# Wider first loads, a later sink-score step and moved DMA transposes in a fused window-attention and SwiGLU kernel

## The chip, the cores and the metric

One core of a Trainium2 chip runs the kernel. The metric is the device time of one execution in microseconds (us); lower is better. Three runs of the kernel before gave 272.84, 273.07 and 273.93 us, the median is 273.07 us.

## What is computed

The reference, cut to what matters (B, H, S, D = 4, 8, 768, 64; 4 sink tokens, a window of 128; d_model 512, d_ff 1536; all f32):

```python
scores = (1.0 / np.sqrt(D)) * np.matmul(q, k.transpose(0, 1, 3, 2))
keep = (pos[None, :] < n_sink) | ((rel >= 0) & (rel < window))   # rel = query position - key position
a = softmax(np.where(keep, scores, -1e9))
attn = np.matmul(a, v)
x = attn.transpose(0, 2, 1, 3).reshape(B * S, H * D)
g = x @ w_gate
out = (g / (1.0 + np.exp(-g))) * (x @ w_val) @ w_out
```

Each query sees at most 128 keys of its window and the 4 first keys (the sinks) of its sequence.

## The kernel before

The 3072 tokens are 12 groups of 256 (three to each of the four sequences). The attention of a group g is a row of steps: `step_T` (L234) turns k and q to the layout [head dim, token] with TensorE transposes and evicts them into `kT`, `qT`; `step_S` (L275) makes the scores of the window, the exponentials on ScalarE (L297) and puts off a multiplication by the mask on VectorE (L302); `step_K` (L306) makes the scores of the sinks from `kss`, four keys per head that `step_ks` (L262) copied out of `kT`; `step_PV` (L318) multiplies by v and normalises into `xn`; `step_X` (L351) turns `xn` into `xT`, the input of the feed-forward part. From group 4 on, k, q and x are not turned on TensorE but by DMA transposes, all of them issued on SP's queue: `xbar(g)` (L253) issues four of them, from `nat` to `kT` and `qT`, and `step_X` one for each 128 tokens (L360).

The feed-forward part works on eight blocks of 256, 256, 256, 512, 512, 512, 512 and 256 tokens: `gate` (L373) for the two first products (`pg`, tanh in `th`, `pv`, then `u` and `ht` on VectorE), `down` (L406) for the last product, its eviction `ot` on ScalarE and the output's DMA on SP's queue (L424). Block 3 holds groups 3 and 4, block 5 groups 7 and 8.

The order of the work is written by hand. `weave(us, slots(...))` goes through a list of units (gates and downs) and calls the attention steps of a slot inside the unit with that number: in a gate between `pg` and `pv`, in a down between its matmuls. Each engine and each DMA queue works through its instructions in program order. Loads with a cast from f32 to bf16 are issued on POOL's queue in the order k and q of groups 0 and 1, v of group 0 (`va`), the first gate and value weights (`wg`, `wv`), and so on (L180 to L200). A DMA on POOL's queue takes one of eight semaphores in turn, and waits until the DMA that had it eight places earlier has landed; SP's and ACT's DMAs share eight others in the same way.

Group 0 is special. Its heads 0 to 3 (pairs 0 and 1 of two heads) are loaded as f32 by SP (k) and ACT (q), one DMA for each pair, and cast by VectorE (L517) and ScalarE (L518); pairs 2 and 3 are cast by four DMAs of POOL (`pair_by_cast`, L180). In all eight a partition holds four tokens of one head, the two heads of a pair stand in the two halves of the partitions, and the access pattern of the source has the two heads as its outermost dimension:

```python
return src[0, 2 * p:2 * p + 2, 0:256].rearrange("w (m r) d -> w m (r d)", r=4)
```

`pair_T` (L479) transposes a pair with sixteen 64x64 matmuls (L486). `fill` issues eight matmuls on zeros ahead of it.

Of the kernel before, what the change touches and what calls it, by code (L numbers as in the profile page):

```python
# [7 lines left out]
FP32 = mybir.dt.float32  # L8
BF16 = mybir.dt.bfloat16
# [5 lines left out]
def kernel(  # L15
# [12 lines left out]
    nc = tc.nc  # L28
    P = 128
    B, H, S, D = q.shape  # L30
# [22 lines left out]
    def pool(name, bufs, psum=False):  # L53
        if psum:
            return ctx.enter_context(
                tc.tile_pool(name=name, bufs=bufs, space=bass.MemoryType.PSUM))
        return ctx.enter_context(tc.tile_pool(name=name, bufs=bufs))

    const = pool("const", 1)
    wpool = pool("wpool", 1)  # L60
    rowp = pool("rowp", 3)
    natp = pool("natp", 3)
    stp = pool("stp", 4)
    vpool = pool("vpool", 1)
    kqtp = pool("kqtp", 2)
    epool = pool("epool", 2)
# [12 lines left out]
    def bank(shape, dtype, name):  # L79
        return psum.tile(shape, dtype, tag="b", name=name)  # L80


    rows, nats, vas = {}, {}, {}
# [8 lines left out]
    def new_rows(g):  # L92
        rows[g] = rowp.tile([P, 2, NP2, 4 * D], BF16, tag="rows", name="rows")
        return rows[g]

    def load_rows(g, pairs=ALL, tensors=(0, 1)):
        b, c = divmod(g, GC)
        x = rows[g] if g in rows else new_rows(g)
        for i in tensors:
            for w in range(2):  # L100
                nc.gpsimd.dma_start(
                    x[64 * w:64 * (w + 1), i, pairs],
                    by_rows((k, q)[i], b, w, pairs, c * 256))
# [39 lines left out]
    ident = const.tile([P, P], BF16)  # L143
# [20 lines left out]
    nc.vector.memset(kss, 0.0)  # L164


    def by_pair(src, p):
        return src[0, 2 * p:2 * p + 2, 0:256].rearrange("w (m r) d -> w m (r d)", r=4)

    new_rows(0)  # L170
    first = {}
    for p in range(2):
        for i, eng in ((0, nc.sync), (1, nc.scalar)):
            st = stp.tile([P, 4 * D], FP32, tag="st", name="st")
            eng.dma_start(st, by_pair((k, q)[i], p))
            first[p, i] = st
    nc.scalar.activation(warmed, one, AF.Exp)

    def pair_by_cast(p, i):
        nc.gpsimd.dma_start(rows[0][:, i, p], by_pair((k, q)[i], p))  # L180

    pair_by_cast(2, 0)
    nc.gpsimd.iota(tq, [[1, P]], base=0, channel_multiplier=0,
                   allow_small_or_imprecise_dtypes=True)
    nc.gpsimd.iota(tk, [[0, 1]], base=0, channel_multiplier=1,
                   allow_small_or_imprecise_dtypes=True)
    pair_by_cast(2, 1)
    pair_by_cast(3, 0)
    pair_by_cast(3, 1)
    load_rows(1)  # L190
    load_v(0)
    load_gate(0)
# [21 lines left out]
    for p in range(NP2):  # L214
        for w in range(2):
            h = 2 * p + w
# [12 lines left out]
    def new_T(b):  # L229
        if b not in kTs:  # L230
            kTs[b] = kqtp.tile([P, NP2, S], BF16, tag="kT", name="kT")
            qTs[b] = kqtp.tile([P, NP2, S], BF16, tag="qT", name="qT")
# [29 lines left out]
    def step_ks(b):  # L262
        for h in range(2):
            r = slice(h * D, (h + 1) * D)
            nc.vector.tensor_copy(
                out=kss[r, b, :, h * NS:(h + 1) * NS], in_=kTs[b][r, :, 0:NS])
        vsb = const.tile([P, H, D + 1], BF16, tag=f"vsb{b}", name="vsb")
        nc.vector.tensor_tensor(
            vsb,
            vcf[:, b:b + 1].broadcast_to([P, H, D + 1]),  # L270
            diag_h.rearrange("q (h o) -> q h o", o=1).broadcast_to([P, H, D + 1]),
            op=ALU.mult)
        vsbs.append(vsb)
# [32 lines left out]
    def step_K(g):  # L306
        b, c = divmod(g, GC)
        if c == 0:
            return
        ps = bank([P, 256], FP32, "pk")  # L310
        for p in range(NP2):
            nc.tensor.matmul(
                ps[32 * p:32 * p + KW], kss[:, b, p], qTs[b][:, p, c * 256:(c + 1) * 256],
                start=True, stop=True, skip_group_check=True)
        es_t[g] = espool.tile([P, 256], BF16, tag="es", name="es")
        nc.scalar.activation(es_t[g], ps, AF.Exp, scale=scale)
# [113 lines left out]
    def gates(tb):  # L430
        return [(gate, tb, f) for f in range(0, DFC, 512 // SIZES[tb])]

    def downs(tb):
        return [(down, tb, t) for t in range(SIZES[tb] // P)]

    def A(fn, *a):
        return lambda: fn(*a)

    def T(g):
        return [A(step_T, g, i, p2) for p2 in range(2) for i in range(2)]  # L440

    def Ss(g):
        return [A(step_S, g, p2) for p2 in range(2)]

    def PVs(g):
        return [A(step_PV, g, j, hh) for hh in range(2) for j in range(2)]

    def Xs(g):
        return [A(step_X, g, j) for j in range(2)]

    def K(g):
        return A(step_K, g)

    def weave(us, slots):
        assert all(i < len(us) for i in slots)
        for i, (fn, tb, x) in enumerate(us):
            fn(tb, x, slots.get(i, []))
# [7 lines left out]
    def slots(*pairs):  # L465
        sl = {}
        for at, steps in pairs:
            for i, step in zip(at if isinstance(at, tuple) else (at,) * len(steps),
                               steps):
                sl.setdefault(i, []).append(step)  # L470
        return sl
# [7 lines left out]
    def pair_T(p, key_eng):  # L479
        new_T(0)  # L480
        pt = bank([P, 2, 256], FP32, "pt")
        for i in range(2):
            for r in range(4):
                for w in range(2):
                    h = slice(64 * w, 64 * (w + 1))
                    nc.tensor.matmul(  # L486
                        pt[h, i, r:256:4], rows[0][h, i, p, r * D:(r + 1) * D],
                        ident[h, h], start=True, stop=True, skip_group_check=True)
        if key_eng == "a":
            nc.scalar.copy(out=kTs[0][:, p, 0:256], in_=pt[:, 0])  # L490
        else:
            nc.vector.tensor_copy(out=kTs[0][:, p, 0:256], in_=pt[:, 0])
        nc.vector.tensor_copy(out=qTs[0][:, p, 0:256], in_=pt[:, 1])
# [20 lines left out]

    fill(8, bank([P, 512], FP32, "w"))
    for p in range(2):
        nc.vector.tensor_copy(out=rows[0][:, 0, p], in_=first[p, 0])  # L517
        nc.scalar.copy(out=rows[0][:, 1, p], in_=first[p, 1])  # L518
        pair_T(p, "a")
    pair_S(0, 1)  # L520
    pair_T(2, "v")
    pair_S(1)
    pair_mask(0)
    pair_T(3, "v")
    pair_S(2, 1)
    pair_mask(1)
# [8 lines left out]
    masks1 = list(later)  # L535
# [13 lines left out]

    nc.vector.tensor_scalar(lt8, th8, float(NS), None, op0=ALU.is_lt)  # L550
    nc.vector.scalar_tensor_tensor(diag_h, th8, 0.0, lt8, op0=ALU.is_ge, op1=ALU.mult)
    for m in masks1[:2]:
        m()
    step_ks(0)
    for m in masks1[2:]:
        m()
    step_K(1)
    load_rows(3)
    load_v(3)

# [5 lines left out]
    def L(*fs):  # L566
        def f():
            for x in fs:
                x()
        return f  # L570

    weave(us, slots(
        (1, PVs(1) + Xs(1)),
        ((5, 5, 6, 6), T(2)), ((7, 8), Ss(2)), (8, [K(2)]),
        ((9, 9, 10, 10), PVs(2)), (11, Xs(2)),
        (12, [L(A(load_nat, 4), A(load_v, 4), A(load_nat, 5), A(load_v, 5),
                A(load_nat, 6), A(load_v, 6))]),
        ((13, 14, 15, 16), T(3)), ((17, 18), Ss(3)), (18, [A(step_ks, 1)]),
        (18, [A(xbar, 4)]),
        ((19, 19, 20, 20), PVs(3)), (21, Xs(3)),  # L580
        ((20, 21), Ss(4)), (21, [K(4)]), (22, [A(xbar, 5)]),
        ((22, 22, 23, 23), PVs(4)), (23, Xs(4))))

    def pair(ga, gb, sh=0):
        s = sh
        return [((s, s + 2), Ss(ga)), (s + 2, [K(ga)]),
                ((s + 4, s + 5, s + 6, s + 7), PVs(ga)),
                ((s + 6, s + 8), Ss(gb)), ((s + 8, s + 9), Xs(ga)), (s + 8, [K(gb)]),
                ((12, 12, 13, 13) if s else (10, 11, 12, 13), PVs(gb)),
                ((14, 14) if s else (13, 14), Xs(gb))]  # L590

    weave(gates(3) + downs(3), slots(
        (0, [L(A(load_nat, 7), A(load_v, 7))]), (2, [A(xbar, 6)]),
        (2, [L(A(load_nat, 8), A(load_v, 8))]), (5, [A(step_ks, 2)]), *pair(5, 6),
        (8, [A(xbar, 7)]), (9, [L(A(load_nat, 9), A(load_v, 9))]),
        (14, [A(xbar, 8)]), (14, [L(A(load_nat, 10), A(load_v, 10))])))
    weave(gates(4) + downs(4), slots(
        *pair(7, 8), (8, [A(xbar, 9)]), (9, [A(step_ks, 3)]),
        (9, [L(A(load_nat, 11), A(load_v, 11))]), (13, [A(xbar, 10)])))
    weave(gates(5) + downs(5), slots(*pair(9, 10), (6, [A(xbar, 11)])))  # L600
    us = gates(6) + gates(7) + downs(6) + downs(7)
    us[-1] = (lambda tb, t, a: down(tb, t, a, True), *us[-1][1:])
# [37 lines left out]
```

## Time and profile before

| | |
|---|---|
| median of three runs | 273.07 us |
| the profiled execution | 273.33 us |
| its span, first to last instruction | 271.5 us |
| PE busy | 240.5 us (89%) |
| VectorE busy | 165.6 us (61%) |
| ScalarE busy | 109.8 us (40%) |
| mean granted share of the TensorE clock | 0.987 |
| chain that ended last: PE, DVE, DMA, SP's queue | 74%, 9%, 9%, 3% |

The chain is followed back from the last instruction: at each step to what released it. A share of 74% for PE means that for 74% of the span the last thing to be waited for was a matmul; the rest is where another engine or a transfer was. A row of idle time names the engine that waited and what ended its wait.

### The profile page before, as it was taken

How to read it: one execution, taken by the hardware profiler on the slowest of the kernel's cores; microseconds unless marked ns; L12 is line 12 of the kernel's file. 1: busy time of each engine (PE TensorE's matmuls, PEld its weight loads, DVE VectorE, ACT ScalarE, POOL GpSimd, SP SyncE). 2: the span in 40 equal slices, each digit the busy share in tenths (PEclk: the TensorE clock that was granted, in tenths of full speed). 3: DMA queues.
4: the chain of work that ended last, by engine and by line, in shares of the span. 5: the costliest groups of instructions: out<-in, count | busy, mean ns of one | idle time of the engine just before them, and what ended most of it. 6: DMA issues, size and time to landing. Idle time of an engine off the chain costs nothing.

```text
span 271.5 us, 5112 instructions
## 1 busy us (share of the span) xinstructions
PE 240.5 (89%) x2016; PEld 138.4 (51%) x2039; DVE 165.6 (61%) x347; ACT 109.8 (40%) x213; POOL 71.1 (26%) x93
## 2 busy tenths in 40 slices
PE   5039679999999958999999999969999999999995
PEld 1026468877865523454444545424545445568543
DVE  4016977788686503899608899117898058977300
ACT  2016613733365414554138471235461265233122
POOL 8139665399450052491006100000000000000000
PEclk9999999999999997999999999988999999999999
DMA  3949999999995379999149910462010320000122
GB/s 35 127 50 145 190 187 206 203 161 150 128 156 70 114 133 197 151 145 115 58 116 163 130 39 4 108 186 57 0 39 2 116 77 2 19 22 0 39 91 105
DMA packets 102960, 27.38 MB, mean 101 GB/s; under 512 B 88985, under 2 KB 99993, under 8 KB 102937
## 3 DMA queue, kind: packets, MB, share of 16 engines
q0 software_dynamic: 72544, 13.91, 65.2%
q1 hardware_dynamic: 30132, 12.89, 20.3%
q8 instruction: 16, 0.26, 0.4%
q10 hardware_dynamic: 260, 0.26, 0.3%
q14 instruction: 8, 0.06, 0.1%
HBM read 28.34 MB, written 6.29 MB: 128 GB/s over the span
## 4 chain that ended last, share of the span: by engine, by line
PE 74%; DVE 9%; DMA 9%; SPq 3%; ACT 3%; issue 2%; DVEq 0%; ACTq 0%
PE pv L388 22%; PE pg L388 21%; PE pd L419 19%; DMA st<-in_k_dram 6%; PE o L336 4%; PE s L290 4%; DMA xT<-xn 2%; DVE ht L402 2%; DVE xn L342 2%; SPq L259 2%; PE pt L244 2%; ACT e L297 1%; DVE e L302 1%; DVE u L401 1%; PE pt L486 1%
## 5 line engine op out<-in xcount | busy, mean ns | idle before, releaser
L388 PE MATMUL pg<-xT,wg 128*128 128x256 bf16 (+1 forms) x380 | 75.3, 329 | 6.7 <-DMA xT<-xn 6.5
L395 ACT ACTIVATE th<-pg 128x512 f32<-128x512 f32 x72 | 43.4, 603 | 83.8 <-PE pg L388 83.3
L388 PE MATMUL pv<-xT,wv 128*128 128x256 bf16 (+1 forms) x374 | 74.9, 328 | 1.4 <-DVE ht L402 0.8
L401 DVE SCALAR_TENSOR_TENSOR u<-th,pg 128x512 bf16<-128x512 f32 x72 | 49.2, 683 | 42.6 <-ACT th L395 42.3
L419 PE MATMUL pd<-wo,ht 128*128 128x512 bf16 (+1 forms) x291 | 65.0, 370 | 0.6 <-issue 0.2
L402 DVE TENSOR_TENSOR ht<-u,pv 128x512 bf16<-128x512 bf16 x72 | 49.5, 688 | 12.5 <-PE pv L388 6.4
L388 PEld LDWEIGHTS <-wg 128*128 128x128 bf16 x384 | 37.6, 99 | 33.0 <-issue 6.1
L388 PEld LDWEIGHTS <-wv 128*128 128x128 bf16 x384 | 34.5, 98 | 21.5 <-issue 4.0
L297 ACT ACTIVATE e<-s 128x512 bf16<-128x512 f32 (+1 forms) x88 | 42.9, 580 | 3.6 <-PE s L290 3.5
L419 PEld LDWEIGHTS <-ht 128*128 128x128 bf16 x300 | 28.1, 98 | 28.6 <-issue 0.3
L423 ACT ACTIVATE ot<-pd 128x512 f32<-128x512 f32 (+1 forms) x25 | 14.6, 583 | 50.9 <-PE pd L419 50.9
L111 POOL DMA_DIRECT2D nat<-in_k_dram x16 | 14.2, 903 | 55.5 <-DMA qT<-nat 50.9
L302 DVE TENSOR_TENSOR e<-e,mask 128x1024 bf16<-128x1024 bf16 (+1 forms) x44 | 26.9, 649 | 2.9 <-ACT e L297 2.9
L122 POOL DMA_DIRECT2D va<-in_v_dram x24 | 21.5, 913 | 16.1 <-DMA rows<-in_k_dram 8.2
L342 DVE TENSOR_TENSOR xn<-o,rcp 128x256 bf16<-128x256 f32 x48 | 20.4, 425 | 1.7
L336 PEld LDWEIGHTS <-e 128*128 128x128 bf16 x352 | 16.5, 98 | 6.3 <-issue 0.2
L336 PE MATMUL o<-va,e 128*128 128x65 bf16 x352 | 17.8, 193 | 0.0
L486 PE MATMUL pt<-ident,rows 64*64 64x64 bf16 x64 | 4.2, 341 | 12.6 <-DVE rows L517 12.6
L111 POOL DMA_DIRECT2D nat<-in_q_dram x16 | 14.3, 919 | 0.0
L290 PE MATMUL s<-qT,kT 64*128 64x128 bf16 (+1 forms) x240 | 13.6, 246 | 0.2 <-DVE qT L251 0.2
L341 DVE RECIPROCAL rcp<-o 128x4 f32<-128x4 f32 x48 | 8.5, 177 | 6.9 <-PE o L336 6.7
L290 PEld LDWEIGHTS <-kT 64*128 64x128 bf16 x240 | 8.1, 97 | 7.8 <-issue 7.1
(57 smaller groups left out, 102.7 us busy)
## 6 DMA issues: line engine op xcount, KB each, us to landing
out_dram<-ot SPq DMA_DIRECT2D x23, 256.0 KB
va<-in_v_dram POOLq DMA_DIRECT2D x24, 128.0 KB, 7.0
nat<-in_k_dram POOLq DMA_DIRECT2D x16, 128.0 KB, 6.0
nat<-in_q_dram POOLq DMA_DIRECT2D x16, 128.0 KB, 6.5
wo<-in_moe_w_out_dram POOLq DMA_DIRECT2D x4, 384.0 KB, 11.6
wg<-in_moe_w_gate_dram POOLq DMA_DIRECT2D x4, 256.0 KB, 7.0
wv<-in_moe_w_val_dram POOLq DMA_DIRECT2D x4, 256.0 KB, 7.5
rows<-in_k_dram POOLq DMA_DIRECT2D x6, 128.0 KB, 13.2
```

Of the source, the lines that this page charges most:

```text
L111: nc.gpsimd.dma_start(x[:, i, j].rearrange("p (h d) -> p h d", d=D), src[b, :, t0:t0 + P].rearrange("h p d -> p h d"))
L122: nc.gpsimd.dma_start(va[:, j, :, 0:D], v[b, :, t0:t0 + P].rearrange("h p d -> p h d"))
L290: nc.tensor.matmul(pss[2 * pp + h][:, col:col + n], kTs[b][r, p, kk:kk + P], qTs[b][r, p, qq:qq + n], start=True, stop=True)
L297: nc.scalar.activation(e_t[g][:, h0 + h, lo:512], pss[2 * pp + h][:, lo:512], AF.Exp, scale=scale)
L302: nc.vector.tensor_tensor(e, e, m[:, :, lo:512].broadcast_to([P, 2, 512 - lo]), op=ALU.mult)
L336: nc.tensor.matmul(o, l, r, start=(i == 0), stop=(i == len(mms) - 1), skip_group_check=True)
L342: nc.vector.tensor_tensor(xns[g, j][:, 256 * hh:256 * (hh + 1)].rearrange("p (h d) -> p h d", h=4), po[:, :, 0:D], rcp.broadcast_to([P, 4, ...
L388: nc.tensor.matmul(ps[:, i * n:(i + 1) * n], ws[fi][:, c, fo * P:(fo + 1) * P], x[:, c], start=(c == 0), stop=(c == DMC - 1))
L395: nc.scalar.activation(th, pg, AF.Tanh, scale=0.5)
L401: nc.vector.scalar_tensor_tensor(u, th, 1.0, pg, op0=ALU.add, op1=ALU.mult)
L402: nc.vector.tensor_tensor(hts[tb][:, f:f + two].rearrange("p a n -> p (a n)"), u, pv, op=ALU.mult)
L419: nc.tensor.matmul(po, hts[tb][:, f, ts * P:(ts + 1) * P], wos[f // n][:, f % n, lo:hi], start=(f == 0), stop=(f == DFC - 1))
```

## The change

Three things change. First, group 0's k and q come with two tokens per partition, all heads side by side (`x0`), in four DMAs of four heads each: heads 0 to 3 as f32 on SP and ACT, heads 4 to 7 by cast on POOL. The source's outermost dimension is now the 128 token pairs, its pieces are half as long (128 elements, not 256). `pair_T` takes eight matmuls of 128 columns instead of sixteen of 64. Second, `step_K(1)`, which stood ahead of the first gate, moves into the first gate between `pg` and `pv`, and `step_ks(0)` ahead of all four mask multiplications of group 1. Third, the calls of `xbar` and of some `load_nat`, `load_v` move to other slots.

```diff
-    def by_pair(src, p):
-        return src[0, 2 * p:2 * p + 2, 0:256].rearrange("w (m r) d -> w m (r d)", r=4)
+    def by_two(src, h0):
+        return src[0, h0:h0 + 4, 0:256].rearrange("h (m r) d -> m h (r d)", r=2)
+    x0 = const.tile([P, 2, H, 2 * D], BF16)
...
-    for p in range(2):
-        for i, eng in ((0, nc.sync), (1, nc.scalar)):
-            st = stp.tile([P, 4 * D], FP32, tag="st", name="st")
-            eng.dma_start(st, by_pair((k, q)[i], p))
+    for i, eng in ((0, nc.sync), (1, nc.scalar)):
+        st = stp.tile([P, 4, 2 * D], FP32, tag="st", name="st")
+        eng.dma_start(st, by_two((k, q)[i], 0))
...
-    pair_by_cast(2, 0)
+    nc.gpsimd.dma_start(x0[:, 0, 4:8], by_two(k, 4))
...
-    pair_by_cast(2, 1)
-    pair_by_cast(3, 0)
-    pair_by_cast(3, 1)
+    nc.gpsimd.dma_start(x0[:, 1, 4:8], by_two(q, 4))
...
-            for r in range(4):
+            for r in range(2):
                 for w in range(2):
-                    h = slice(64 * w, 64 * (w + 1))
                     nc.tensor.matmul(
-                        pt[h, i, r:256:4], rows[0][h, i, p, r * D:(r + 1) * D],
-                        ident[h, h], start=True, stop=True, skip_group_check=True)
+                        pt[64 * w:64 * (w + 1), i, r:256:2],
+                        x0[:, i, 2 * p + w, r * D:(r + 1) * D], ident,
+                        start=True, stop=True, skip_group_check=True)
...
-    for m in masks1[:2]:
-        m()
     step_ks(0)
-    for m in masks1[2:]:
+    for m in masks1:
         m()
-    step_K(1)
...
-        (1, PVs(1) + Xs(1)),
+        (0, [K(1)]), (1, PVs(1) + Xs(1)),
...
-        (18, [A(xbar, 4)]),
+        (15, [A(xbar, 4)]), (18, [A(xbar, 5)]),
...
-        ((20, 21), Ss(4)), (21, [K(4)]), (22, [A(xbar, 5)]),
+        ((20, 21), Ss(4)), (21, [K(4)]),
...
-        (9, [L(A(load_nat, 11), A(load_v, 11))]), (13, [A(xbar, 10)])))
+        (3, [L(A(load_nat, 11), A(load_v, 11))]), (15, [A(xbar, 10)])))
```

In the units of block 3 `xbar(6)` moves from slot 2 to 1, `xbar(7)` from 8 to 6, the loads of group 9 from 9 to 7, `xbar(8)` and the loads of group 10 from 14 to 15; in those of block 4 `xbar(9)` and the loads of group 11 go to slot 3 (from 8 and 9).

POOL's queue at the start, before: four loads of one pair (`rows`, L180), then group 1 (`rows`, L101), v (`va`), the first weights.

```order
L180 DMA rows<-in_k_dram 128x1x256
L183 ISA
L183 IOTA tq 128x128
L185 IOTA tk 128x1
L180 DMA rows<-in_q_dram 128x1x256
L180 DMA rows<-in_k_dram 128x1x256
L180 DMA rows<-in_q_dram 128x1x256
L101 DMA rows<-in_k_dram 64x4x256 x2
L101 DMA rows<-in_q_dram 64x4x256 x2
L122 DMA va<-in_v_dram 128x8x64 x2
L132 DMA wg<-in_moe_w_gate_dram 128x4x256
```

The same queue now:

```order
L179 DMA x_127<-in_k_dram 128x4x128
L180 ISA
L180 IOTA tq 128x128
L182 IOTA tk 128x1
L184 DMA x_127<-in_q_dram 128x4x128
L101 DMA rows<-in_k_dram 64x4x256 x2
L101 DMA rows<-in_q_dram 64x4x256 x2
L122 DMA va<-in_v_dram 128x8x64 x2
L132 DMA wg<-in_moe_w_gate_dram 128x4x256
```

Two loads (`x_127` is `x0`) stand for four, so that the two `va` of group 0 are the seventh and eighth DMA and no longer the ninth and tenth: they wait for no semaphore, and `wg` for that of `x0`'s k.

SP's queue ahead of block 3, before: `nat_1065` is group 5 (the end of `xbar(5)`), `xT_1453` the two x transposes of group 4, `nat_1074` group 6.

```order
L259 DMA_TRANSPOSE qT_1108<-nat_1065 128x4x128
L259 DMA_TRANSPOSE kT_1107<-nat_1065 128x4x128
L259 DMA_TRANSPOSE qT_1108<-nat_1065 128x4x128
L424 DMA out_0_dram<-ot_1553 128x512
L360 DMA_TRANSPOSE xT_1453<-xn_1519 128x4x128
L360 DMA_TRANSPOSE xT_1453<-xn_1536 128x4x128
L424 DMA out_0_dram<-ot_1597 128x512
```

Now (`nat_1027` is group 5, `xT_1419` the x transposes of group 4):

```order
L254 DMA_TRANSPOSE kT_1069<-nat_1027 128x4x128
L254 DMA_TRANSPOSE qT_1070<-nat_1027 128x4x128
L419 DMA out_0_dram<-ot_1354 128x512
L419 DMA out_0_dram<-ot_1413 128x512
L419 DMA out_0_dram<-ot_1471 128x512
L419 DMA out_0_dram<-ot_1515 128x512
L355 DMA_TRANSPOSE xT_1419<-xn_1479 128x4x128
L355 DMA_TRANSPOSE xT_1419<-xn_1497 128x4x128
L419 DMA out_0_dram<-ot_1559 128x512
```

`xbar(5)` stands ahead of the first four outputs, so that only an output is left just ahead of the x transposes.

SP's queue ahead of block 5, before: `nat_2074` is group 10, `xT_2382` the x transposes of group 8.

```order
L360 DMA_TRANSPOSE xT_2382<-xn_2443 128x4x128
L259 DMA_TRANSPOSE kT_2390<-nat_2074 128x4x128
L259 DMA_TRANSPOSE qT_2391<-nat_2074 128x4x128
L259 DMA_TRANSPOSE kT_2390<-nat_2074 128x4x128
L259 DMA_TRANSPOSE qT_2391<-nat_2074 128x4x128
L424 DMA out_0_dram<-ot_2554 128x512
L360 DMA_TRANSPOSE xT_2382<-xn_2472 128x4x128
L424 DMA out_0_dram<-ot_2571 128x512
```

Now (`xT_2359` is group 8's, `nat_2051` group 10):

```order
L355 DMA_TRANSPOSE xT_2359<-xn_2405 128x4x128
L419 DMA out_0_dram<-ot_2512 128x512
L355 DMA_TRANSPOSE xT_2359<-xn_2434 128x4x128
L419 DMA out_0_dram<-ot_2529 128x512
L254 DMA_TRANSPOSE kT_2172<-nat_2051 128x4x128
L254 DMA_TRANSPOSE qT_2173<-nat_2051 128x4x128
L254 DMA_TRANSPOSE kT_2172<-nat_2051 128x4x128
L254 DMA_TRANSPOSE qT_2173<-nat_2051 128x4x128
L419 DMA out_0_dram<-ot_2549 128x512
```

The four transposes of `xbar(10)` stood between the two x transposes of group 8 and now stand behind both.

## Rows read from the trace of the kernel before

**Rows 1.** Waits of all engines: engine line <- releaser: us in total, times, longest us.

```profile
PE pt L486 <- DVE rows L517: 12.6, 2, 8.3
PE pg L388 <- DMA xT<-xn: 6.5, 2, 4.0
```

**Rows 2.** Chain that ended last, pieces of the span: start us, us, what.

```profile
1.51 16.60 DMA st<-in_k_dram
...
98.45 4.28 DMA xT<-xn
...
178.17 2.32 DMA xT<-xn
```

**Rows 3.** Stretches of the span: length, engines' busy us, PEclk, DMA share, GB/s written.

```profile
2.00:3.00 1.00, 1.00 (x4) 0.39 (x3) 0.36 (x3) 0.56 (x1) 0.91 (x4) 1.00 0.20 8
13.00:17.00 4.00, 1.06 (x16) 0.82 (x16) 0.49 (x2) 0.78 (x2) 0.92 (x1) 1.00 0.15 41
28.50:36.00 7.50, 4.93 (x75) 3.78 (x76) 7.17 (x20) 3.89 (x8) 4.19 (x7) 1.00 1.44 195
75.00:82.00 7.00, 6.95 (x68) 4.55 (x67) 6.33 (x14) 4.26 (x10) 3.50 (x4) 1.00 2.43 156
```

**Rows 4.** Timeline of VectorE at the start: start us, us, instruction [idle before <-releaser].

```profile
12.78 0.29 DVE L517 CAST rows<-st 128x256 bf16<-128x256 f32 x1 [8.46 <-DMA st<-in_k_dram]
14.63 0.42 DVE L493 CAST qT<-pt 128x256 bf16<-128x256 f32 x1 [1.56 <-ACT kT L490]
```

**Rows 5.** Timeline of PE at the start: transposes of pairs 0, 1 and 2.

```profile
13.12 1.06 PE L486 MATMUL pt<-ident,rows 64*64 64x64 bf16 x16 [8.30 <-DVE rows L517]
18.48 1.06 PE L486 MATMUL pt<-ident,rows 64*64 64x64 bf16 x16 [4.30 <-DVE rows L517]
...
20.45 1.06 PE L486 MATMUL pt<-ident,rows 64*64 64x64 bf16 x16
```

**Rows 6.** Timeline of POOL's queue: loads and what they waited for.

```profile
1.25 0.97 POOL L180 DMA_DIRECT2D rows<-in_k_dram  x1 [0.81 <-POOLq L621]
...
15.71 0.92 POOL L122 DMA_DIRECT2D va<-in_v_dram  x1 [8.21 <-DMA rows<-in_k_dram]
19.18 0.88 POOL L122 DMA_DIRECT2D va<-in_v_dram  x1 [2.55 <-DMA rows<-in_q_dram]
...
38.63 3.01 POOL L139 DMA_DIRECT2D wo<-in_moe_w_out_dram  x4 [1.10 <-DMA rows<-in_k_dram]
...
98.09 1.76 POOL L111 DMA_DIRECT2D nat<-in_k_dram  x2 [19.60 <-DMA qT<-nat]
```

**Rows 7.** Timeline of PE: the first transposes of group 2.

```profile
44.64 1.08 PE L244 MATMUL pt<-ident,rows 64*64 64x64 bf16 x32
```

**Rows 8.** Stretch in which PE waits for `kss` (columns as in Rows 3).

```profile
30.00:36.00 6.00, 3.70 (x58) 3.12 (x58) 5.76 (x16) 2.69 (x6) 3.47 (x5) 1.00 1.45 196
```

**Rows 9.** Timeline ahead of block 3: eviction of an output, last `xn` of group 4.

```profile
93.00 0.60 ACT L423 ACTIVATE ot<-pd 128x512 f32<-128x512 f32 x1 [2.21 <-PE pd L419]
...
94.80 0.42 DVE L342 TENSOR_TENSOR xn<-o,rcp 128x256 bf16<-128x256 f32 x1
```

**Rows 10.** Timeline of PE: the first matmuls of blocks 3 and 5, and scores of group 10.

```profile
102.86 1.87 PE L388 MATMUL pg<-xT,wg 128*128 128x512 bf16 x4 [4.00 <-DMA xT<-xn]
...
180.53 1.15 PE L388 MATMUL pg<-xT,wg 128*128 128x512 bf16 x3 [2.51 <-DMA xT<-xn]
...
195.02 0.62 PE L290 MATMUL s<-qT,kT 64*128 64x128 bf16 x12
```

**Rows 11.** Stretches behind these two waits: length, PE busy, PEclk, DMA share, GB/s.

```profile
102.90:106.10 3.20, 3.20 (x18) 0.50 1.89 211
181.40:184.60 3.20, 3.20 (x15) 0.50 0.59 154
```

**Rows 12.** Timeline ahead of block 5: eviction of an output, last `xn` of group 8.

```profile
171.15 0.42 DVE L342 TENSOR_TENSOR xn<-o,rcp 128x256 bf16<-128x256 f32 x1
...
172.88 0.60 ACT L423 ACTIVATE ot<-pd 128x512 f32<-128x512 f32 x1 [2.35 <-PE pd L419]
```

More of the change, by code (lines that the diff above doesn't have):

```diff
@@ L62 @@
     natp = pool("natp", 3)
-    stp = pool("stp", 4)
+    stp = pool("stp", 2)
     vpool = pool("vpool", 1)
@@ L164 @@
     nc.vector.memset(kss, 0.0)
-    def by_pair(src, p):
-        return src[0, 2 * p:2 * p + 2, 0:256].rearrange("w (m r) d -> w m (r d)", r=4)
-    new_rows(0)
-    first = {}
-    for p in range(2):
-        for i, eng in ((0, nc.sync), (1, nc.scalar)):
-            st = stp.tile([P, 4 * D], FP32, tag="st", name="st")
-            eng.dma_start(st, by_pair((k, q)[i], p))
-            first[p, i] = st
+    def by_two(src, h0):
+        return src[0, h0:h0 + 4, 0:256].rearrange("h (m r) d -> m h (r d)", r=2)
+    x0 = const.tile([P, 2, H, 2 * D], BF16)
+    first = []
+    for i, eng in ((0, nc.sync), (1, nc.scalar)):
+        st = stp.tile([P, 4, 2 * D], FP32, tag="st", name="st")
+        eng.dma_start(st, by_two((k, q)[i], 0))
+        first.append(st)
     nc.scalar.activation(warmed, one, AF.Exp)
-    def pair_by_cast(p, i):
-        nc.gpsimd.dma_start(rows[0][:, i, p], by_pair((k, q)[i], p))
-    pair_by_cast(2, 0)
+    nc.gpsimd.dma_start(x0[:, 0, 4:8], by_two(k, 4))
     nc.gpsimd.iota(tq, [[1, P]], base=0, channel_multiplier=0,
@@ L516 @@
     for p in range(2):
-        nc.vector.tensor_copy(out=rows[0][:, 0, p], in_=first[p, 0])
-        nc.scalar.copy(out=rows[0][:, 1, p], in_=first[p, 1])
+        h = slice(2 * p, 2 * p + 2)
+        nc.vector.tensor_copy(out=x0[:, 0, h], in_=first[0][:, h])
+        nc.scalar.copy(out=x0[:, 1, h], in_=first[1][:, h])
         pair_T(p, "a")
@@ L551 @@
     nc.vector.scalar_tensor_tensor(diag_h, th8, 0.0, lt8, op0=ALU.is_ge, op1=ALU.mult)
-    for m in masks1[:2]:
-        m()
-    step_ks(0)
-    for m in masks1[2:]:
-        m()
-    step_K(1)
+    step_ks(0)
+    for m in masks1:
+        m()
     load_rows(3)
@@ L592 @@
     weave(gates(3) + downs(3), slots(
-        (0, [L(A(load_nat, 7), A(load_v, 7))]), (2, [A(xbar, 6)]),
+        (0, [L(A(load_nat, 7), A(load_v, 7))]), (1, [A(xbar, 6)]),
         (2, [L(A(load_nat, 8), A(load_v, 8))]), (5, [A(step_ks, 2)]), *pair(5, 6),
-        (8, [A(xbar, 7)]), (9, [L(A(load_nat, 9), A(load_v, 9))]),
-        (14, [A(xbar, 8)]), (14, [L(A(load_nat, 10), A(load_v, 10))])))
+        (6, [A(xbar, 7)]), (7, [L(A(load_nat, 9), A(load_v, 9))]),
+        (15, [A(xbar, 8)]), (15, [L(A(load_nat, 10), A(load_v, 10))])))
     weave(gates(4) + downs(4), slots(
-        *pair(7, 8), (8, [A(xbar, 9)]), (9, [A(step_ks, 3)]),
-        (9, [L(A(load_nat, 11), A(load_v, 11))]), (13, [A(xbar, 10)])))
+        *pair(7, 8), (3, [A(xbar, 9)]), (9, [A(step_ks, 3)]),
+        (3, [L(A(load_nat, 11), A(load_v, 11))]), (15, [A(xbar, 10)])))
     weave(gates(5) + downs(5), slots(*pair(9, 10), (6, [A(xbar, 11)])))
```

## The prediction

> **What bounds the kernel now.** PE is busy for 89% of the span, so I read first what the idle PE waits for: transposes of group 0 wait 12.6 us in two pieces for VectorE's cast, and the first matmuls of two feed-forward blocks wait 6.5 us for DMA transposes of x [rows 1]. Nothing else that PE waits for is as long. The chain agrees: it begins with 16.60 us of a k load, and later holds the two x transposes, 4.28 and 2.32 us [rows 2]. So the question is what the change does to these three places, and whether the work behind them can start earlier.
>
> **The start: the loads.** Pair 0 is transposed at 13.12 and pair 1 at 18.48, 0.34 after the cast of its k began [rows 4, 5]; the last k lands at 18.11 [rows 2]. The stretches show why this takes so long: from 13 to 17 us, while that load is under way, the 16 DMA engines are busy for 0.15 of the time, which is 2.4 engines' worth, and 41 GB/s move; later, weight loads whose outermost dimension is the 128 partitions keep a share of 1.44 (requests overlap, so it passes 1) and 195 GB/s [rows 3]. The loads of one pair, two heads outermost, thus sit on few engines. The new loads have the 128 token pairs outermost. The rows can't say that they spread, but their nearest neighbours, all the loads of [rows 3] with partitions outermost, do.
> The Trainium skill goes further, on the page DMA: Bandwidth & Descriptors, section Why a DMA increments its semaphore by 16 and not by 1: a transfer runs on the largest number of engines up to 16 that divides the slowest dimension of both its sides, which makes 2 for the old loads and 16 for the new. The trace's 2.4 agrees with the first; the second no row shows. By this rule the sum is the one below; by the row of 13 to 17 us alone a load as slow as the old stays possible, the rival on spreading below.
>
> k and q of heads 0 to 3 are 512 KB as f32. At the rate that 0.15 of the engines gave, 41 / 0.15 = 273 GB/s, that is 1.9 us; if a piece half as long costs as much as a whole one, 3.8. First bytes move in the third microsecond [rows 3], so from 2.2 k lands at 4.1 to 6.0. The casts of heads 4 to 7 share the engines: 256 KB written, at 195 GB/s (pieces of 512 bytes) to 156 (pieces of 128 bytes, v and k by token [rows 3]) 1.3 to 1.7 us, hence 4.1 to 7.7. I take 5.6, the middle with a part of the sharing.
> On the same page, section Specifications, the skill wants pieces of at least 512 bytes for the full rate, which speaks against this change: the f32 pieces shrink to just that, the casts write 256. By that rule only the casts would pay, and by the rows, between 195 and 156 GB/s, 0.4 us at most, off the path. The sum stays with the rows.
>
> Then pair 0 is transposed at 5.6 + 0.34 = 5.9. Pair 1 no longer waits for a load but for the chain of pair 0, which VectorE works off in order: from the transposes at 13.12 to the end of q's eviction at 14.63 + 0.42 is 1.93, then the cast 0.29 and 0.05 to PE, 2.3 in all [rows 4, 5]. Eight matmuls of 128 columns stream as many columns as sixteen of 64, so I leave their 1.06 as it is. Pair 1 starts at 8.2 instead of 18.48: **10.3 us gained**, with ends 11.8 (landing at 4.1) and 8.2 (7.7).
>
> **What could eat that.** Pair 2 follows pair 1 by 1.97 [rows 5], at 10.2. Its k and q come by POOL's queue, issued at 1.25 and, one load of 0.97 and three small instructions later, 2.7; in the rows that load, on few engines, held POOL until 15.71 [rows 6]. With 7.5 us from issue to need I count no wait. Behind it stands POOL's queue: it was through with its first eight loads at 15.71 - 8.21 = 7.50, and the second `va` went out at 19.18 only [rows 6]. Now two loads of four are gone (0.8 each, a little under the 0.97 of the first) and the two `va` (0.92 + 0.88) wait for nothing: the queue reaches the weights at about 7.7 instead of 20.06, 12.4 earlier, more than PE moves. From there loads stream at the full rate as before, so each keeps its lead; the shortest I find is group 2's k, which landed at 38.6 [rows 6] for transposes at 44.64 [rows 7], 6 us. PE waits for no weight now and should not then.
>
> **The sink scores.** From 30 to 36 us PE idles 6.00 - 3.70 = 2.3 us, all of it ahead of `step_K(1)` for `kss`; but VectorE is busy for 5.76 of these 6.00 [rows 8], and what follows on PE needs its masks and `xn`. The change reorders VectorE's work and removes none, so PE starts its first gate earlier and then waits for the masks instead. I take 0; ends 2.3 gained, 0.3 lost (four small matmuls between `pg` and `pv`).
>
> **Block 3.** PE idles 4.00 us until the x transposes of group 4 have landed, at 102.86 [rows 10]. Behind the wait the granted clock is 0.50, the 1.2 GHz level, for 3.4 us (the stretch 102.9 to 106.1 lies inside), in which PE is busy throughout [rows 11]: 3.4 x 0.5 = 1.7 us more. The second x transpose began at 98.45, behind four transposes of group 5 and an output. Now only an output is ahead, ready at 93.00 + 0.60, and the second `xn` at 94.80 + 0.42 = 95.2 [rows 9]. With the first transpose issued as its `xn` comes, the second starts at about 95.8. It ended 2.32 later in the other place and 4.28 here [rows 2]; the longer ran beside the loads that POOL sent at 98.09 when group 5's transposes had landed [rows 6], and these move ahead with them. 95.8 + 2.4 = 98.2 is before PE's last matmul of block 2 at 98.86: the wait goes, **5.7 us**. At 4.28 it would leave 1.3 us, so the low end is 2.7, with the clock lost again.
>
> **Block 5.** The same with 2.51 us [rows 10] and another 1.7 at the lower clock [rows 11]: the second x transpose began at 178.17 behind `xbar(10)`. Its `xn` was ready at 171.6 and the output now ahead of it at 172.88 + 0.60 = 173.5 [rows 12], so it starts at 174.1 and lands at 176.5, before 178.02 where PE went idle: **4.2 us**, low end 2.5. The moved transposes are hidden: if the four of `xbar(10)` ran one after the other from 176.5 on, at 2.32 each, they would end at 185.8, and the scores of group 10 that need them begin at 195.02 [rows 10], 190.8 by then. If that cover were gone, each us late would stall PE by one.
>
> **The sum.** From the profiled execution's 273.33 us (0.3 above the median of 273.07, inside the runs' spread): 273.3 - 10.3 - 0 - 5.7 - 4.2 = **253.1 us**. Its own ends: 273.3 - 11.8 - 2.3 - 5.7 - 4.2 = 249.3 and 273.3 - 8.2 + 0.3 - 2.7 - 2.5 = 260.2.
>
> **The rivals.**
> - *The x transposes still come late.* Only the place in SP's queue changes, and if what remains in flight beside them sets their landing, PE waits as before: 273.3 - 10.3 = 263.0. Against it speaks the gap of 4 us between ready and issued in block 5.
> - *The start is bound by POOL's loads.* If pair 2's data land as late as the first POOL load now, 15.7, pair 2 starts at 15.8 instead of 20.45: 273.3 - 4.7 - 9.9 = 258.7. For it: these loads took 14 us [rows 6]. Against: on few engines.
> - *The loads don't spread.* With the old engines and the whole of k landing in one load at 18.1, pair 0 starts at 18.4 and pair 1 at 20.7: 2.2 lost, 273.3 + 2.2 - 9.9 = 265.6.
> - *Slower: pieces cost by their number, on the old engines.* The first load has twice as many pieces as the two before. If each costs as much as the longer ones did and few engines carry them, the stretch from 2 to 18.1 us doubles, k lands at 34, pair 1 starts at 36.7, 18.2 later: 273.3 + 18.2 - 9.9 = 281.6. It decides from a landing of k at about 26, where the loss passes the 9.9 of the transposes. Against it: the loads in pieces of 128 bytes reach 156 GB/s against 195 [rows 3], so length matters little where engines are many.
>
> **How the numbers follow.** The forecast has 0.72, the late x transposes 0.10, POOL's loads 0.11, no spreading 0.04, the slower case 0.03. The predicted time is the forecast's, 253.1. The range of 250 to 260 takes its own bounds and the case of POOL's loads and leaves out the rest, 0.17. A measurement of this kernel can tell about 0.5%, 1.4 us, from no change. Faster by more: 0.96; within: 0.01; slower: 0.03.
>
> **What would show it.** In the profile after: the first cast of `st` at 5 to 7 us, both pairs' transposes 2.3 us apart, pair 2 without a wait, a DMA share of about 1 before 10 us; POOL's second `va` by 8 us; no wait of PE for `xT` above 1 us and a granted clock without a stretch at 0.50 behind blocks 2 and 4; PE's wait for `kss` gone and one of the same length for masks in its place. I am wrong if PE waits for weights or rows of group 2, if a landing near 18 us stays, or if the x transposes are issued early and still land late.

## The result and the profile after

The changed kernel takes 252.65 us (250.18 to 253.81, 4 runs), the kernel before 273.06 on the same chip: a ratio of 0.9235 [0.9161 to 0.9309], 20.4 us less by the medians. 253.1 was forecast, 250 to 260. The profiled execution is the fastest of the four, 250.18 us with a span of 247.8; its mean granted clock is 1.000, that of the three others, 252.15 to 253.81 us, 0.986. Ratios and their intervals leave out runs that took over 1.5% more than the fastest of their kernel (three of e3, two of e9 below); the medians keep them.

The waits of PE in the changed kernel (engine, line, tile <- releaser: us in total, times, longest us):

```profile
PE px L360 <- DVE xn L337: 2.9, 5, 1.3
PE w L471 <- DVE zero L161: 1.2, 1, 1.2
PE pt L480 <- DVE x L513: 1.2, 1, 1.2
PE pv L383 <- DVE ht L397: 0.7, 3, 0.3
PE pg L383 <- DVE xT L363: 0.5, 1, 0.5
```

Both lines of [rows 1] are gone: the transposes of group 0 wait 1.2 us instead of 12.6, and there is no wait for a DMA transpose. The chain of the profile has no DMA piece any more where [rows 2] had three:

```profile
PE 85%; DVE 10%; ACT 3%; issue 1%; DVEq 0%
```

The start, from the timelines of VectorE, ScalarE and PE (start us, us, instruction [idle before <- releaser]):

```profile
4.24 0.41 DVE L513 CAST x<-st 128x256 bf16<-128x256 f32 x1
4.59 0.41 ACT L514 CAST x<-st 128x256 bf16<-128x256 f32 x1 [1.86 <-DMA st<-in_q_dram]
4.75 0.87 PE L480 MATMUL pt<-ident,x 128*64 128x128 bf16 x8
...
6.83 0.63 PE L480 MATMUL pt<-ident,x 128*64 128x128 bf16 x8 [1.20 <-DVE x L513]
7.98 0.63 PE L480 MATMUL pt<-ident,x 128*64 128x128 bf16 x8
...
10.86 1.97 PE L239 MATMUL pt<-ident,rows 64*64 64x64 bf16 x64
...
24.52 1.04 PE L383 MATMUL pg<-xT,wg 128*128 128x256 bf16 x8
```

They answer to [rows 4, 5]. The cast of k comes at 4.24 with no wait for data shown, pair 1 at 6.83 instead of 18.48, pair 2 at 7.98 without a wait. The matmuls of a pair take 0.63 instead of 1.06 from pair 1 on. The last two rows, the first transposes of group 1 and the second gate of block 0, were these in the kernel before:

```profile
24.65 1.97 PE L244 MATMUL pt<-ident,rows 64*64 64x64 bf16 x64
...
38.43 1.04 PE L388 MATMUL pg<-xT,wg 128*128 128x256 bf16 x8
```

The stretches (length, busy us of PE, PEld, DVE, ACT and POOL, granted clock, DMA share, GB/s):

```profile
2.00:6.00 4.00, 3.62 (x15) 1.25 (x13) 1.98 (x8) 1.47 (x5) 3.92 (x9) 1.00 1.21 206
...
17.00:24.60 7.60, 4.90 (x65) 3.59 (x65) 7.28 (x22) 1.77 (x4) 4.26 (x7) 1.00 1.45 196
```

Against the share of 0.15 and 41 GB/s of [rows 3], the first loads now come at 1.21 and 206 GB/s. (The trace of this run has no record of the clock before 5.3 us, and the column shows 1.00 there, whatever the level was.) From 17 to 24.6 us VectorE is the bound as it was in [rows 8]: the wait of 2.26 us for `kss` is gone, and in its place PE idles 1.30 us for `xn` ahead of one `px`, where it idled 0.47 before (the 0.81 ahead of the next was there before), 0.51 for `xT` ahead of the first gate and 0.30 for a mask. The second gate of block 0 ends that stretch; it starts at 24.52 here and started at 38.43 before, 13.9 us earlier.

The first matmuls of blocks 3 and 5 on PE, and the x transposes ahead of block 3 in SP's queue:

```profile
80.60 2.74 SPq L355 DMA_TRANSPOSE xT<-xn  x2
...
85.00 1.02 PE L383 MATMUL pg<-xT,wg 128*128 128x512 bf16 x4
...
158.34 1.03 PE L383 MATMUL pg<-xT,wg 128*128 128x512 bf16 x4
```

Neither waits, and four matmuls take 1.02 instead of the 1.87 of [rows 10]. So the gain grows along the span: 13.9 us at the second gate, 102.86 - 85.00 = 17.9 at block 3 (the 4.00 of its wait), 180.53 - 158.34 = 22.2 at block 5 (1.7 of clock and 2.51 of wait), 271.5 - 247.8 = 23.7 at the end (1.5 of clock). That is the best run; the medians differ by 20.4, and the experiments had to say where 3 us go.

### The profile page after: what moved, and what is told of

Read it like the earlier page. It is cut to its first block, busy times and chain, and to the rows that moved or that the text cites. A ratio compares the mean times of both kernels' runs of the same rounds, so it can differ in the third digit from the quotient of the medians.

```text
span 247.8 us, 5063 instructions
## 1 busy us (share of the span) xinstructions
PE 236.3 (95%) x2007; PEld 135.9 (55%) x2007; DVE 165.2 (67%) x347; ACT 109.4 (44%) x213; POOL 69.3 (28%) x91
## 4 chain that ended last, share of the span: by engine, by line
PE 85%; DVE 10%; ACT 3%; issue 1%; DVEq 0%
PE pd L414 25%; PE pv L383 24%; PE pg L383 22%; PE o L331 4%; PE s L285 4%; DVE ht L397 3%; DVE xn L337 2%; PE pt L239 2%; DVE e L297 1%; PE w L471 1%; ACT e L292 1%; DVE u L396 1%; PE pt L480 1%; PE px L360 1%; DVE vsb L263 1%
## 5 line engine op out<-in xcount | busy, mean ns | idle before, releaser
L383 PE MATMUL pg<-xT,wg 128*128 128x256 bf16 (+1 forms) x384 | 74.2, 326 | 0.6 <-DVE xT L363 0.5
L414 PE MATMUL pd<-wo,ht 128*128 128x512 bf16 (+1 forms) x300 | 66.0, 371 | 0.0
L337 DVE TENSOR_TENSOR xn<-o,rcp 128x256 bf16<-128x256 f32 x48 | 20.4, 425 | 1.7
L285 PE MATMUL s<-qT,kT 64*128 64x128 bf16 (+1 forms) x240 | 12.9, 237 | 0.2 <-DVE qT L246 0.2
L331 PE MATMUL o<-vsb,es 128*128 128x260 bf16 x32 | 8.8, 274 | 0.3 <-ACT es L311 0.3
```

The source lines that it names most:

```text
L285: nc.tensor.matmul(pss[2 * pp + h][:, col:col + n], kTs[b][r, p, kk:kk + P], qTs[b][r, p, qq:qq + n], start=True, stop=True)
L331: nc.tensor.matmul(o, l, r, start=(i == 0), stop=(i == len(mms) - 1), skip_group_check=True)
L337: nc.vector.tensor_tensor(xns[g, j][:, 256 * hh:256 * (hh + 1)].rearrange("p (h d) -> p h d", h=4), po[:, :, 0:D], rcp.broadcast_to([P, 4, ...
L383: nc.tensor.matmul(ps[:, i * n:(i + 1) * n], ws[fi][:, c, fo * P:(fo + 1) * P], x[:, c], start=(c == 0), stop=(c == DMC - 1))
L414: nc.tensor.matmul(po, hts[tb][:, f, ts * P:(ts + 1) * P], wos[f // n][:, f % n, lo:hi], start=(f == 0), stop=(f == DFC - 1))
```

## The experiments

Times are medians; a gain in us is what the ratio lacks to 1, times the time of before on that chip (274.25 for e1 to e4, 273.23 for e5 to e8).

**One part at a time.** From the three parts of the diff, the kernels take these:

```
e1: before + by_two, x0, pair_T and the casts of the diff
e2: before + the new slots of xbar, load_nat and load_v
e3: before + step_ks(0) ahead of masks1, K(1) in slot 0
e4: after, with step_ks(0) behind masks1[:2] and step_K(1) ahead of the gates
```

*e1, the loads alone.*

> The kernel before with the wide loads, their casts and pair_T alone; the sink step and the DMA transposes stay where they were. Theory A (the start pays more than was forecast, because pair 1 starts 11.65 us earlier and the full TensorE clock is there by pair 1): the second gate comes 13.9 us earlier, 273.1 - 13.9 = 259.2 us, 258 to 260.5. Theory B (only what was forecast reaches the end, the rest is eaten by the stretch on VectorE): 273.1 - 10.3 = 262.8. Theory C (the loads behind them, weights and group 2, take back a part): above 265, with a wait of PE for a weight or for rows.

Measured: 261.78 us, 0.9562 [0.9525, 0.9599], 12.0 us less (11.0 to 13.0). The waits for x transposes grew from 6.5 us to 8.0, and the one of block 3 from 4.00 to 5.41 (the waits of PE, then its timeline):

```profile
PE pg L382 <- DMA xT<-xn: 8.0, 2, 5.4
```

```profile
92.46 1.87 PE L382 MATMUL pg<-xT,wg 128*128 128x512 bf16 x4 [5.41 <-DMA xT<-xn]
```

Between A and B. In the profiled run, e1's slowest with 263.14 us, the second gate comes at 26.62, 11.8 us earlier and not 13.9: pairs 2 and 3 take 1.06 and 1.02 there, the time of the lower level, and so the full clock that A counts on isn't there. At block 3 another 1.4 us are lost to transposes that don't move forward as far. The wait for weights or rows of C isn't there.

*e2, the transposes alone.*

> The kernel before with the moved DMA transposes and the loads that belong to them alone. Theory A (both waits for xT go and the clock does not fall behind them): 273.1 - 9.9 = 263.2 us, no wait of PE for xT, no stretch at 0.50 near 103 and 181 us. Theory B (the waits go, the clock falls elsewhere): 273.1 - 6.5 = 266.6. Theory C (in the changed kernel the waits went only because everything runs earlier against the loads): 4 us or more of wait for xT are left, 269 or more.

Measured: 264.03 us, 0.9644 [0.9607, 0.9681], 9.8 us less (8.8 to 10.8). No wait for `xT` is left. The first four matmuls of blocks 3 and 5 take 1.03 us, so the clock doesn't fall behind these places. Theory A holds with its size: stalls and clock are worth 9.8 us behind a late start, and 10.0 behind an early one (from e1 to e4 below, 261.78 to 251.73).

*e3 and e4, the sink scores.*

> The kernel before with the sink scores of group 1 behind the first gate alone. Theory A (VectorE is the bound of that stretch): 273.1 us, within 0.5; the wait for kss goes and waits of about 2 us for masks or xn come in its place. Theory B (the wait for kss was on the path): 270.8, with the second gate 2.3 us earlier.

> The changed kernel with only the sink scores put back to their old place. Theory A: as the changed kernel, 252.6 us by its median, within 1. Theory B (the place of the sink scores is worth 2.3 us once the loads are early): 254.9 or more.

Measured: e3 274.76 us, 1.0009 [0.9977, 1.004]; e4 251.73 us, 0.9196 [0.9162, 0.9229]. Theory A both times. In e3 the waits of PE show the exchange, 2.3 us for `kss` gone and `px` grown from 1.9 to

```profile
PE px L365 <- DVE xn L342: 3.1, 6, 1.3
```

with 0.5 more for `xT` ahead of the first gate and 0.3 for a mask.

The parts add up: 12.0 + 9.8 = 21.8, and e4, which has both, gains 22.0 (21.1 to 23.0).

**Why the loads are early.**

```diff
 e5 (after):
-        eng.dma_start(st, by_two((k, q)[i], 0))
+        for h in range(4):
+            eng.dma_start(st[:, h], (k, q)[i][0, h, 0:256].rearrange(
+                "(m s r) d -> s m (r d)", s=2, r=2))
 e6 (after, rows[0], its casts and pair_T as before):
+        for w in range(2):
+            eng.dma_start(st[64 * w:64 * (w + 1)],
+                          by_rows((k, q)[i], 0, w, slice(0, 2), 0))
```

> The changed kernel, its f32 loads of k and q for heads 0 to 3 in pieces of 512 bytes as there, but one load for each head, with the two alternating sets of 64 partitions outermost, so that the outermost dimension is 2 as in the kernel before (pairs 0 and 1 are transposed from that token order). Theory A (the outermost dimension sets how many DMA engines carry a load): the 512 KB move at the 41 GB/s of the kernel before, 12.8 us, pair 1 starts at about 15 us instead of 6.83, 252.6 + 8 = 260.6 us; a DMA share of about 0.15 for these loads. Theory B (pieces and their length set it, not the outermost dimension): k lands as in the changed kernel plus the issue of six more loads on two queues, pair 1 by 8.5, 254.5 at most.

Measured: 270.66 us, 0.9872 [0.9837, 0.9907]. The two casts of k in VectorE's timeline show how late pieces of the same length land when the outermost dimension is 2; the third row is pair 1 on PE:

```profile
10.93 0.29 DVE L517 CAST x<-st 128x256 bf16<-128x256 f32 x1 [6.80 <-DMA st<-in_k_dram]
...
21.76 0.29 DVE L517 CAST x<-st 128x256 bf16<-128x256 f32 x1 [5.94 <-DMA st<-in_k_dram]
...
22.11 0.64 PE L482 MATMUL pt<-ident,x 128*64 128x128 bf16 x4 [7.16 <-DVE x L517]
```

Pair 1 started at 22.11, 15.3 us later than in the changed kernel and 3.6 later than before. So A has the direction but not the size (15 us and 260.6 were expected), and B is excluded: SP has issued all four loads of k by 7.03, and the last of them lands only at 21.7. The pieces themselves are no slower than the old ones. Over the first 24 us the packets of one of the two tensors took 3.7% of the 16 engines' time in e5 (520 packets), 3.6% before (260) and 3.6% in the changed kernel (528), some 14 us each time, so a piece of half the length takes half as long. What delays e5 beyond A isn't settled; POOL's queue moved 2.22 MB in these 24 us and 1.31 MB before, so its loads, which are also why no share of 0.15 is seen, may hold up the two engines. The packets of the queue that carries one of the two tensors, from the pages of the changed kernel and of e5 (packets, MB, share of 16 engines):

```profile
q10 hardware_dynamic: 528, 0.26, 0.4%
```

```profile
q10 hardware_dynamic: 520, 0.26, 0.3%
```

528 is 512 pieces and 16 packets, 520 is four loads of 128 pieces and 2, and the 260 of before two loads of 128 and 2. By the Trainium skill, page DMA: Bandwidth & Descriptors, section Why a DMA increments its semaphore by 16 and not by 1, each engine that a load of this queue uses adds one packet for the semaphore, so the surplus counts the engines: 16, and 2. The trace's counts agree, which the rows before could not show.

> The changed kernel with the four tokens and 1 KB pieces of the kernel before, but loaded by head parity onto 64 partitions, 64 outermost, two loads for each tensor; pairs are transposed with 16 matmuls of 64 rows as before. Theory A (spreading is what counts, not two tokens per partition): k lands within 1 us of the changed kernel, pair 1 starts by 7.8, 252.6 within 1.3 us. Theory B (the two-token layout over all 128 partitions matters by itself): pair 1 2 us or more later, 254.6 or more.

Measured: 255.63 us, 0.9334 [0.93, 0.9368], some 3 us longer than the changed kernel. B's numbers hold, pair 1 2.5 us later and a time above 254.6. k is cast 2.2 us later, and then pairs 0 and 1 run at the lower clock:

```profile
6.41 0.35 DVE L510 CAST rows<-st 128x256 bf16<-128x256 f32 x1 [1.99 <-DMA st<-in_k_dram]
...
9.35 1.06 PE L479 MATMUL pt<-ident,rows 64*64 64x64 bf16 x16 [1.47 <-DVE rows L510]
```

Its queue has 288 packets, two loads of 128 pieces and 16, so it spreads as the changed kernel does. Spreading is most of the gain (pair 1 is 9.1 us earlier than before), the form of the loads another 2.5: in the changed kernel one over 128 partitions instead of two over 64, two tokens per partition instead of four, and two of POOL's instead of four, which e6 brings back too. These weren't taken apart. SP issues the second load of k from 1.54 to 2.36, where the changed kernel is through at 1.20, 1.2 us later; what makes up the rest isn't settled.

**The clock at the start.**

```diff
 e7 (after):
-    fill(8, bank([P, 512], FP32, "w"))
 e8 (before):
-    fill(8, bank([P, 512], FP32, "w"))
+    fb = bank([P, 512], FP32, "w")
+    fill(38, fb)
...
+        if p == 1:
+            fill(17, fb)
         pair_T(p, "a")
```

> The changed kernel without the eight fill matmuls ahead of pair 0. Theory A (part of the gain of the start is that the full clock, granted from 5.26 us on because of the fills, now reaches pairs 1 to 3 and the transposes of group 1): pair 0 starts at 4.6 as there, but its followers run at 1.2 GHz, the first transposes of group 1 start at about 13.0 instead of 10.86, and 252.6 + 2 = 254.7 us. Theory B (the clock of these few us does not reach the end): 252.6 within 0.7.

> The kernel before with 38 fill matmuls instead of 8 ahead of pair 0 and 17 more ahead of pair 1, which bridge its two waits for loads. Theory A (clock): from pair 1 at 18.4 on PE runs at 2.4 GHz, the first transposes of group 1 start at 22.5 instead of 24.65, and the kernel takes 2 us less than before, 272. Theory B (the waits of the stretch on VectorE behind it take that back): as before within 0.7.

Measured: e7 252.78 us, 0.9237 [0.9206, 0.9269], no different from the changed kernel. e8 271.94 us, 0.9945 [0.9914, 0.9977], 1.5 us less than before (0.6 to 2.3). The first transposes of group 1 on PE in e7, a stretch of e7 in the columns above, and those transposes in e8:

```profile
12.53 1.97 PE L239 MATMUL pt<-ident,rows 64*64 64x64 bf16 x64
```

```profile
25.00:28.20 3.20, 2.54 (x15) 1.84 (x16) 1.88 (x7) 0.00 (x0) 3.18 (x5) 0.51 1.94 178
```

```profile
22.57 1.97 PE L244 MATMUL pt<-ident,rows 64*64 64x64 bf16 x64
```

From pair 1 to there e8 needs 4.05 us and the changed kernel 4.03, but before 6.17: A is right that a PE kept busy makes these steps 2.1 us shorter, and in e8 1.5 us of that reach the end. In e7 it does not show: its transposes of group 1 start 1.67 us later than in the fastest run of the changed kernel, but that kernel's median is 2.5 us above that run. Where the median loses this, the next run was for; it is the changed kernel itself.

> The changed kernel again, for a profile of a run that is not its fastest. Theory A (the 3 us between its runs are TensorE's clock in the stretch in which PE waits for VectorE): such a run spends 6 to 7 us at 0.50 between 15 and 27 us, which costs 3.4, and is the same elsewhere; runs at a mean clock of 1.0 take 250.2, the others 252 to 254. Theory B (DMA or queue noise): the lost time lies elsewhere, beside waits for data.

Measured: 252.52 us (249.65 to 254.4), 0.9209 [0.9169, 0.9249]; its one run at a mean clock of 1.000 is the 249.65, those at 0.986 took 252.35 and 252.69. Of the two at 0.993 one took 250.86 and the other 254.4, the longest of all, which the mean clock does not explain. The profiled run, 253.63 us at 0.980, has two stretches at half clock, one behind the wait ahead of pair 1 and one from the end of the stretch in which PE waits for VectorE:

```profile
7.30:10.60 3.30, 3.30 (x29) 1.59 (x25) 1.55 (x4) 1.95 (x5) 3.30 (x5) 0.50 1.82 162
10.70:24.30 13.60, 10.56 (x190) 7.56 (x188) 12.15 (x33) 7.72 (x17) 9.54 (x15) 1.00 1.57 189
24.40:31.10 6.70, 5.91 (x31) 4.24 (x32) 3.38 (x9) 0.60 (x1) 4.90 (x8) 0.50 1.60 191
```

Each of its waits of PE is within 0.4 us of the best run's. So A in the main: 6.7 us at 0.50, in which PE is busy for 5.91, cost about 3. They come from 24.4 to 31.1 and not between 15 and 27, and the first stretch is one that A did not have; the transposes of group 1 start at 11.98 there instead of 10.86. One stretch of 6.7 us makes a mean of 0.987 over 250 us, and the five runs at 0.986, of this row and of the result, take 2.9 us more on average than the two at 1.000; but none of the five was profiled. e4 has such a drop too, from 18.0 to 24.6, and e7 the row above. The best run has the same waits ahead of it and no drop, so the idle PE alone does not bring it. What less of it does was tried next.

**A version with less of that idle time.** The `px` of group 1 don't block the second gate any more:

```diff
 e10 (after):
         def dve():
             nc.vector.tensor_copy(out=xTs[tb][:, :, off:off + P], in_=pt)
+        if g == 1:
+            nc.scalar.copy(out=xTs[tb][:, :, off:off + P], in_=pt)
+            return
...
-        (0, [K(1)]), (1, PVs(1) + Xs(1)),
+        (0, [K(1)]), (1, PVs(1)), (2, Xs(1)),
 e11 (e10): both casts of both pairs ahead of pair_T(0)
         nc.scalar.copy(out=x0[:, 1, h], in_=first[1][:, h])
+    for p in range(2):
         pair_T(p, "a")
 e12 (e11): sk and mask0 behind these casts, fill(7) for fill(8)
```

> The changed kernel with the x transposes of group 1 inside the second gate of block 0, between its pg and its pv, instead of ahead of it, and their evictions on ScalarE instead of VectorE. Theory A (PE idles 1.30 + 0.81 us there only because its queue holds the px matmuls that wait for VectorE's xn; the gate's matmuls do not need them): the pg of 0.87 us fills a part and ScalarE takes 0.89 us off VectorE, 1.2 us less by the profiles, more if the clock then stays up. Theory B (VectorE's chain comes out again as a wait of pv or of the first gate of block 1): same as the changed kernel within 0.7.

> The reordered kernel of the run before, with the casts of both first pairs issued ahead of the transposes of pair 0. Theory A (pair 1 waits for the chain of pair 0 on VectorE and ScalarE, not for data, since one load brings both): pair 1 starts right behind pair 0 at about 5.8 us instead of 6.9, the wait of 1.1 us goes and the time is 250.6 - 1.1 = 249.5 us. Theory B (behind it the chain of pairs 2 and 3 and the loads of group 1 bind): pair 1 starts earlier, the first transposes of group 1 do not, 250.6 within 0.5.

> The kernel with the casts first, with the 0.62 us of VectorE's work on mask0 behind these casts and seven fill matmuls instead of eight. Theory A (k has landed before VectorE is free at 4.15): the first cast starts at 3.7 to 4.0 without a wait for data and the time falls by another 0.3 us. Theory B (k lands at 4.1 to 4.2, as VectorE comes free): VectorE waits for the load and the time is as in the run before.

Measured: e10 250.61 us (250.53 to 251.47), 0.9187 [0.9163, 0.9212]; e11 249.47 us, 0.9114 [0.9077, 0.9151]; e12 249.95 us, 0.9139 [0.9091, 0.9187]. In e10 PE does the gate's `pg` while it would have waited, and its waits for `xn` fall from 2.9 to 2.0 us (PE's timeline, and a stretch in the columns above):

```profile
8.91 1.06 PE L484 MATMUL pt<-ident,x 128*64 128x128 bf16 x8
...
13.28 2.02 PE L239 MATMUL pt<-ident,rows 64*64 64x64 bf16 x64
...
23.70 1.04 PE L387 MATMUL pg<-xT,wg 128*128 128x256 bf16 x8
25.17 0.28 PE L360 MATMUL px<-ident,xn 128*128 128x128 bf16 x2 [0.43 <-DVE xn L337]
...
86.33 1.03 PE L387 MATMUL pg<-xT,wg 128*128 128x512 bf16 x4
```

```profile
7.30:10.60 3.30, 3.30 (x29) 1.49 (x27) 1.01 (x3) 1.41 (x4) 3.30 (x5) 1.00 1.87 164
```

All five of its runs have a mean clock of 0.999 or 1.000, where the changed kernel has two of ten. That mean leaves the start out: the column shows 1.00 in a stretch in which the pairs take 1.06 us each and PE does the same 29 matmuls as in e9 at 0.50. So this run lost 2.42 us up to the transposes of group 1 (13.28 for 10.86). From there to block 3 it needs 73.05 us and the best run of the changed kernel 74.14, 1.1 less, close to A's 1.2. But all five of its times lie above the two of the changed kernel at 1.000, and its interval overlaps that kernel's. So the gain in that stretch and the steadier clock behind the start are shown, the cause of the steadier clock and a gain in the kernel's time are not.

e11 has the time of its theory A, 249.5, and its interval lies below both intervals of the changed kernel. Pair 1 there follows pair 0 at once, and the transposes of group 1 start at 9.71 instead of 10.86:

```profile
4.71 1.25 PE L484 MATMUL pt<-ident,x 128*64 128x128 bf16 x16
...
85.18 1.02 PE L387 MATMUL pg<-xT,wg 128*128 128x512 bf16 x4 [2.27 <-DMA xT<-xn]
```

The second row is from its slowest run, the one profiled, and shows what is late next: block 3 comes early enough to wait for its x transposes again. The second of them takes 4.37 us from issue to landing there, like the 4.28 of [rows 2]. e12 waits 1.28 at the same place, in a run of 249.66. It also settles when k lands, since there VectorE is free earlier and waits:

```profile
4.20 0.65 DVE L513 CAST x<-st 128x256 bf16<-128x256 f32 x2 [0.55 <-DMA st<-in_k_dram]
```

That is theory B: k lands at about 4.2 us, and the masks in front of the cast cost nothing that the runs show.

## Why the prediction was right, and where it was not

- **The cause of the late start: right.** The forecast took the few engines to be the reason, from a row of 0.15 of the engines; e5 puts them back, with four loads for one, and pair 1 falls to 22.1 us with everything else of the change in place. e6 spreads them in another form and keeps 9.1 of the 11.65 us at pair 1.
- **The start, 10.3 us: too small by 3.6 in the profiled run.** k was taken to land at 5.6, between its bounds of 4.1 and 7.7, and lands at 4.2, near the low end; that is 1.4 at pair 1 (6.83 for 8.2). The upper bounds had two reasons. That a half piece may cost as much as a whole one is not so (the packets took some 14 us with either), and k lands too early for sharing with POOL's casts to have cost it much. The step "eight matmuls of 128 columns stream as many columns as sixteen of 64, so I leave their 1.06" holds for the columns (both forms take 1.06 at the one level and 0.63 at the other) but took the clock as unchanged: behind the fills and without the long waits pairs 1 to 3 run at 0.63, and 2.1 us more are there at the transposes of group 1. e8 gets the same 2.1 in the old order. In other runs part of it (e1, e9) or all of it (e10) is missing.
- **A term that was missing, some 3 us the other way.** The median lies 2.5 us above the fastest run. In the three profiles e4, e7 and e9 the clock is at 0.50 for 3.2 to 6.7 us in or behind the stretch in which PE waits for VectorE, and eight of the changed kernel's ten runs have a mean below 1.000. The forecast priced the clock behind the two x transposes and nowhere else. That the median came out within 0.5 us of 253.1 is luck: this and the start nearly cancel.
- **The sink scores, 0: right** (e3, e4). PE waits elsewhere instead, as described, though mostly for `xn` and `xT` and only 0.3 us for a mask, where the forecast expected one wait for masks.
- **Blocks 3 and 5, 5.7 and 4.2: right.** Together 9.9 were forecast; e2 measures 9.8 with them alone, and the profile has 4.0 and 4.3 up to block 5 and 1.5 behind it.
- **The rivals.** Late x transposes did not come in the changed kernel, but the slack was thin: PE waits longer for them in e1, where they stand in the old order, and again in e11 and e12, in the new order; 2.4 us from issue to landing, as the forecast took, is not sure. POOL's loads bind nowhere; the second `va` is out by 7.5 us. The case of slow pieces fails twice: the change leaves the few engines, and e5, which puts them back, has the last k at 21.7, short of the 26 from which it would have decided, with pieces that cost by their bytes and not by their number.

## What to carry to other kernels

Read a load that takes long by the share of DMA engines in its stretch before its bytes or its piece length: here the outermost dimension of the access pattern, with four loads for one, was worth 15 us at pair 1. Where PE queues matmuls that wait for a slower engine, put work that needs nothing ahead of them; it filled 1.1 us of the wait here, and whether it keeps the clock up is open. Look for the clock's level in the time of equal matmuls too, not only in its mean. A start that is moved forward is worth only as much as the transfers further on have slack, so look at the next wait for data too.

## What was not expected

The same kernel has another clock from run to run, and much of its spread goes with it: the changed kernel took 249.65 us at a mean of 1.000 and 252.35 to 252.69 at 0.986, though its longest run, 254.4, had 0.993. And spread loads come later beside slow ones. The first weight load of POOL's queue, the same in both kernels, took 6.6 us from issue to landing in the changed kernel and 17.3 in e5 (DMA issues: KB each, median us to landing):

```profile
wg<-in_moe_w_gate_dram POOLq DMA_DIRECT2D x1, 256.0 KB, 6.6
```

```profile
wg<-in_moe_w_gate_dram POOLq DMA_DIRECT2D x1, 256.0 KB, 17.3
```

So loads on few engines can delay more than themselves. That the spread loads wait there for the few busy engines is likely but not shown, and PE waits for no weight in e5.
